# Gated mix of two state-space layers: work on GpSimd, VectorE and the DMA queues moved at three edges of the kernel

## The chip, the cores and the metric

The kernel runs on one core of a Trainium2 chip. TensorE multiplies matrices, VectorE and ScalarE work on tiles, GpSimd (POOL in the profile) works on tiles too and issues DMAs that add into their target, and SyncE (SP) issues the plain and the transposing DMAs. Each of them runs its own instructions in order. The metric is the device time of one execution in microseconds (us); lower is better. The kernel before took a median of 427.84 us over three runs (427.82 to 430.52).

## The reference

x is one sequence of 2048 rows and 1024 columns in bf16. The result is `g * a + (1 - g) * b`, where g is a gate per row, a is a linear recurrence over time with 1024 complex states, and b is a long convolution per column.

```python
g = sigmoid((x * gate_w).sum(-1, keepdims=True))

# a: the recurrence
dt = exp(log_dt); Lam = Lambda_re + 1j * Lambda_im
Lam_bar = exp(dt * Lam)
B_bar = ((Lam_bar - 1.0) / Lam)[:, None] * Bmat
Bu = einsum("bld,pd->blp", x, B_bar)
for t in range(L):
    h = Lam_bar * h + Bu[:, t, :]
a = 2.0 * einsum("blp,dp->bld", hseq, Cmat).real + x * Dskip

# b: the convolution (q is x here)
k_shift = sum over t of k_pad[:, t:t + S, :] * shift_k[:, ks - 1 - t]      # ks = 4
kv = k_shift * v
y = irfft(rfft(kv, 2 * S) * rfft(ssm_k, 2 * S))[:, :S, :] + kv * ssm_D
b = x * y

out = g * a + (1 - g) * b
```

## The kernel before, in words

**The convolution** is done for one block of 128 columns at a time, c from 0 to 7 (`NC` is 8), as matrix products with cosine and sine tables. For one c:

- `load` puts k (transposed, tile `kT`), the long filter (`kn`) and v into SBUF, by SyncE's queue.
- `taps` makes the four-tap sums on TensorE, and ScalarE copies them to `ks`. `times_v` multiplies by v on VectorE, mirrors the result on TensorE, copies the mirror to `lo` on ScalarE, makes the difference `ev` on VectorE and the sum by a DMA from GpSimd's queue that adds `lo` into `ks` (line 485). `first_times_v` does the same for c = 0 with VectorE alone. `fold_K` does it for the filter.
- `fwd_K` and `fwd_V` transform both, in two halves `hf`; ScalarE copies the results to `Kh` and `Vh`.
- `products` multiplies the two spectra on VectorE into the tile `G`. It is a generator that is advanced by hand: step 1 writes the first product into `G`; step 2 makes `n1` and adds it into `G` by a DMA from GpSimd's queue (line 544); step 3 makes `t2`; step 4 makes and adds the others; step 5 adds the last `n1` into `G`, and needs the DMA's result; the rest finishes `G`. p0 is half 0, p1 is half 1, whose last steps run in the next c.
- `inverse` multiplies `G` with the tables `CI` and `SI` on TensorE (`psz`); ScalarE copies the result to `cv`, and SyncE stores it to a scratch buffer in DRAM.

The tables `CI` and `SI` come from `inverse_angles` and `inverse_table`, in two halves; each half of the table is three large ScalarE instructions (Abs, Sin, Sin).

**The factors of the states.** `state_params` (lines 330 to 385) makes the decay, the angles, the sines and cosines and the complex factor `c2r`, `c2i` of each state, on tiles of 128x8. `turn_table` then makes one table of turns per block of 128 states, in steps: ScalarE scales a row of times by the angle (`hr`), VectorE reduces it in two operations, ScalarE takes sine and cosine (`TCS`), then scales them into `m` (one buffer, `m_pool`) and into `TCSi`, and a DMA of GpSimd's queue adds `m` to `TCSi`.

**The recurrence** runs on blocks of 512 times (tb from 0 to 3) and groups of 256 states (g from 0 to 3). `Bu` multiplies x (transposed, tiles `xT`, one for each tb) with `BT[g]` on TensorE. `scan` turns it with `TCSi` (`A`), runs the decay with VectorE's scan instruction (`W`), and turns back (`hb`). `Cy` multiplies `hb` with `CT` into a row block of 128 times (`psy`), and `scale_a` scales that by the gate on ScalarE. `loads` fetches the convolution's result (`pbb`) and x (`xr`) for a row block, `scale_b` scales `pbb` and makes `gd` from `drow` (Dskip on all partitions), which a DMA adds to `pbb`. `finish` multiplies the two on VectorE, adds the scaled `psy` and stores the rows. The last four row blocks have their sums of `Cy` over g interleaved, since all need the last scan.

**Order.** `put` chains every instruction behind the one that was put on the same engine before, so the order on each engine is the order of the Python text. PSUM holds four tiles of 128x1024, used in turn (`ps2`): TensorE can start a tile when the one four places before has been read. What the change touches is in three places: the loop over c for c = 0 (with the lines just ahead of it), the loop's last turn with the stage for c = 7 that follows, and the last four row blocks.

SyncE's queue, in order, around the second place: `xT` of block 1 (two transposes, line 813), `BT[2]` (two), the two stores of `cv`, `drow` (line 875), `BT[3]` (two), the stores of `inverse(6)`, of `inverse(7)`, `xT` of block 2, 16 transposes for `CT`, then the first `loads`.

Of the kernel before, what the change touches and what calls it, by code (L numbers as in the profile page):

```python
# [9 lines left out]
ALU = mybir.AluOpType  # L10
# [10 lines left out]
def kernel(  # L21
# [71 lines left out]
    def put(eng, f, *a, **kw):  # L93
        with tc.issue_after(prev[eng]) if eng in prev else nullcontext():
            i = f(*a, **kw)  # L95
        prev[eng] = getattr(i, "ins", i)
# [9 lines left out]
    def tt(o, a, b, op):  # L106
        put("dve", V.tensor_tensor, out=o, in0=a, in1=b, op=op)

    def ts(o, a, s1, s2, op0, op1=None):
        if op1 is None:  # L110
            put("dve", V.tensor_scalar, out=o, in0=a, scalar1=s1, scalar2=None, op0=op0)
        else:
            put("dve", V.tensor_scalar, out=o, in0=a, scalar1=s1, scalar2=s2, op0=op0, op1=op1)

    def copy(o, a):
        put("dve", V.tensor_copy, o, a)
# [213 lines left out]
    def state_params():  # L330

        dtv = small("dtv")
        act(dtv, logdt, func=ACT.Exp)
        av = small("av")
        tt(av, dtv, Lre, ALU.mult)
        bv = small("bv")
        tt(bv, dtv, Lim, ALU.mult)
        act(rv, av, func=ACT.Exp)
        ts(thn, bv, 1.0 / TWO_PI, None, ALU.mult)
        yield  # L340
        thU = small("thU")
        ts(thU, thn, float(TB), None, ALU.mult)
        frs = []
        for x, name in ((thn, "th"), (thU, "thU")):
            rq = small(name + "_rq")
            ts(rq, x, MAGIC, -MAGIC, ALU.add, ALU.add)
            fr = small(name + "_fr")
            tt(fr, x, rq, ALU.subtract)
            frs.append(fr)
        sc = []  # L350
        for fr, name in zip(frs, ("th", "thU")):
            fa = small(name + "_fa")
            act(fa, fr, func=ACT.Abs)
            s_ = small(name + "_sin")
            act(s_, fr, func=ACT.Sin, scale=TWO_PI)
            c_ = small(name + "_cos")
            act(c_, fa, func=ACT.Sin, bias=pih, scale=-TWO_PI)
            sc += [s_, c_]
        sth, cth, cs["sU"], cs["cU"] = sc
        yield  # L360
        rc = small("rc")
        tt(rc, rv, cth, ALU.mult)
        rs = small("rs")
        tt(rs, rv, sth, ALU.mult)
        nre = small("nre")
        ts(nre, rc, -1.0, None, ALU.add)
        den = small("den")
        tt(den, Lre, Lre, ALU.mult)
        den2 = small("den2")
        tt(den2, Lim, Lim, ALU.mult)  # L370
        tt(den, den, den2, ALU.add)
        invden = small("invden")
        put("dve", V.reciprocal, invden, den)
        ts(invden, invden, 2.0, None, ALU.mult)
        t_a = small("t_a")
        t_b = small("t_b")
        tt(t_a, nre, Lre, ALU.mult)
        tt(t_b, rs, Lim, ALU.mult)
        tt(t_a, t_a, t_b, ALU.add)
        tt(c2r, t_a, invden, ALU.mult)  # L380
        tt(t_a, rs, Lre, ALU.mult)
        tt(t_b, nre, Lim, ALU.mult)
        tt(t_a, t_a, t_b, ALU.subtract)
        tt(c2i, t_a, invden, ALU.mult)
        ts(mc2i, c2i, -1.0, None, ALU.mult)

    def turn_table(pi, home):

# [86 lines left out]
    def times_v(c):  # L475

        ks, v = kss[c], lds.pop(("v", c))
        tt(ks, ks, v.rearrange("p (b q) d -> p q b d", q=4), ALU.mult)
        yield
        lo = eo_pool.tile([128, 2, 4, 128], BF16, name="lo")  # L480
        act(lo, mirror(c), func=ACT.Copy)
        yield
        e = eo_pool.tile([128, 2, 4, 128], BF16, name="ev")
        tt(e, ks[:, 2:4], lo, ALU.subtract)
        gather(ks[:, 2:4], lo)
        eos["v", c] = e, ks[:, 2:4]

    def fwd_K(c, hf):
# [32 lines left out]
            act(Vp[:, :, :, f2], ps, func=ACT.Copy, scale=2.0 / 1024.0)  # L521
        VH[c, hf] = Vp

    def products(c, hf, home=u4):

        K, Vt = KH.pop((c, hf)), VH.pop((c, hf))
        G = g_pool.tile([128, 2, 4, 2, 128], BF16, name="G")

        def mult(a, k, home=w4, t=None):

            full = [128, 2, 4 - a, 256]
            if t is None:
                t = home(full, BF16, "t")
            Ka = K[:, k:k + 1, a:a + 1].rearrange("p c b f d -> p c b (f d)")
            tt(t, bc(Ka, full), Vt[:, :, 0:4 - a].rearrange("p c b f d -> p c b (f d)"), ALU.mult)
            return t

        def at(a):
            return G[:, :, a:4].rearrange("p c b f d -> p c b (f d)")

        mult(0, 0, t=at(0))
        yield
        n1 = mult(1, 0, home)
        gather(at(1), n1)
        yield
        t2 = mult(0, 1, home)
        yield
        n2 = mult(1, 1)
        n3 = mult(2, 1)
        tt(t2[:, :, 1:], t2[:, :, 1:], n2, ALU.add)  # L550
        n2 = mult(3, 1)
        tt(t2[:, :, 2:], t2[:, :, 2:], n3, ALU.add)
        n1 = mult(2, 0)
        n3 = mult(3, 0)
        tt(t2[:, :, 3:], t2[:, :, 3:], n2, ALU.add)
        tt(n1[:, :, 1:], n1[:, :, 1:], n3, ALU.add)
# [136 lines left out]
        act(gd, drow, func=ACT.Identity, scale=gcols[:, t_:t_ + 1])  # L693
        gather(pbb, gd)

    def Cy_g(tb, tl, ps, g, last, js=range(2)):
        tsl = slice(tl * 128, (tl + 1) * 128)
        for j in js:
            for c in range(2):
                for dh in range(2):  # L700
                    mm(ps[dh], hbs[tb, g][:, c, j, tsl], CT[2 * g + j][:, c, dh * 512:(dh + 1) * 512],
                       g == 0 and j == 0 and c == 0, last and j == 1 and c == 1)
# [18 lines left out]
    def finish(t_, ps=None):  # L721

        rows = slice(t_ * 128, (t_ + 1) * 128)
        pbb, xr = ios.pop(t_)
        tt(xr, xr, pbb, ALU.mult)
        if t_ < NT - 4:
            ga = gas.pop(t_)
            gather(ga, xr)
            yield
        elif ps is None:  # L730
            yield
            ga = gas.pop(t_)
            tt(ga, ga, xr, ALU.add)
        else:
            yield
            ga = a_room(t_)
            for o, i in ps:
                put("dve", V.scalar_tensor_tensor, out=ga[:, o], in0=i, scalar=gcols[:, t_:t_ + 1], in1=xr[:, o],
                    op0=ALU.mult, op1=ALU.add)
        move(of[rows, :], ga)  # L740


    def step(gen):
        next(gen, None)
# [43 lines left out]
    run(turns)  # L788
    run(inverse_angles(1))
    turns = inverse_table(1)  # L790
    p0 = products(0, 0)
    steps(p0, 3)
    tv = times_v(1)
# [8 lines left out]
    for c in range(NC - 1):  # L802
# [5 lines left out]
        if c < 4:  # L808
            load_BT(c // 2, c % 2)
        elif c < 6:  # L810
            load_xT(0, halves=(c - 4,))
        else:
            load_xT(1)
            load_BT(2, 0)
            load_BT(2, 1)
        tabs = turn_table(c - 1, u4) if c else none
        back = inverse(c - 1) if c else none
        if c:
# [5 lines left out]
            run(p1)  # L824
            steps(p0, 2)
            run(tv)
        p1 = products(c, 1)

        fwd_K(n, 0)
        step(p0)  # L830
        if c == 0:
            run(tv)
        if nn < NC:
# [11 lines left out]
        run(p0)  # L845
        if nn < NC:
            taps(nn, dg)
        if c == 0:
            step(sp)
        step(tabs)  # L850
        fwd_K(n, 1)
        step(p1)
        if c == 0:
            run(sp)
        fwd_V(n, 0)
        if nn < NC:
            run(fold_K(nn))
            tv = times_v(nn)
            step(tv)
        if c == 0:  # L860
            run(turns)
        fwd_V(n, 1)
        old = tabs

# [2 lines left out]
    with tc.tile_pool(name="fin", bufs=1, side="right") as fin:  # L867
# [4 lines left out]
            return fin.tile(shape, dt, name=name, tag=f"fin{next(count)}")  # L872

        p0, back = products(c, 0, room), inverse(c - 1)
        move(drow, bc(A_Dskip.rearrange("(o d) -> o d", o=1), [128, D]))
        load_BT(3, 0)
        load_BT(3, 1)
        ta, tb_ = turn_table(NP - 2, room), turn_table(NP - 1, room)
# [17 lines left out]
        step(tb_)  # L896
        run(tb_)
        step(p0)
        p1 = products(c, 1, room)
        steps(p1, 2)  # L900
        step(p0)
        step(p1)
        run(p0)
        Bu(0, 1)
        run(p1)
        Bu(0, 2)
# [13 lines left out]
    load_xT(2, xt2_pool)  # L920
    for pi in range(NP):
        load_CT(pi)
    loads(0)
    Bu(0, 3)
    Bu(1, 0)
# [39 lines left out]
    pss = []  # L965
    for tl in range(4):
        ps = ps2([128, 2, 512], "psy")
        pss.append(([ps[:, 0], ps[:, 1]], [(slice(0, D), flat(ps))]))
    for g in range(NG - 1):
        for tl in range(4):  # L970
            Cy_g(tb, tl, pss[tl][0], g, False)
    run(finish(t0 - 1))
    fins = []
    for tl in range(4):
        fins.append(finish(t0 + tl, pss[tl][1] if tl % 2 else None))
        step(fins[tl])
    for tl in range(4):
        Cy_g(tb, tl, pss[tl][0], NG - 1, False, [0])
    for tl in range(4):
        Cy_g(tb, tl, pss[tl][0], NG - 1, True, [1])  # L980
        if tl % 2 == 0:
            scale_a(t0 + tl, pss[tl][1])
    for tl in (1, 0, 3, 2):
        run(fins[tl])
# [1 line left out]
_INS = ['A_x', 'A_Lambda_re', 'A_Lambda_im', 'A_B_re', 'A_B_im', 'A_C_re', 'A_C_im', 'A_log_dt', 'A_Dskip', 'B_q', 'B_k', 'B_v', 'B_shift_k', 'B_ssm_k', 'B_ssm_D', 'gate_w']  # L986
# [26 lines left out]
```

## Time and profile before

The profiled execution took 431.18 us, with a span of 429.4 us from the first to the last instruction; the granted clock was 1.00.

| | busy us | share of the span | instructions |
|---|---|---|---|
| TensorE matmul (PE) | 411.8 | 96% | 2375 |
| VectorE (DVE) | 403.3 | 94% | 577 |
| ScalarE (ACT) | 249.1 | 58% | 303 |
| GpSimd (POOL) | 61.5 | 14% | 80 |

| stage, us from the start | what runs |
|---|---|
| 0 to 50 | tables, first column block, factors of the states |
| 50 to 184 | the loop over column blocks |
| 184 to 214 | last column block, last tables, first `Bu` |
| 214 to 416 | scans on VectorE, `Bu` and `Cy` on TensorE |
| 416 to 429 | last row blocks |

How to read the views: a line of the timeline has start, length, engine, source line, operation, what it writes and reads, and in brackets the idle time of its engine before it and what ended it. Nearly all instructions carry line 95, that of `put`, so they are told apart by their tiles. A line of the waits has who waited for whom, total us, times and the longest. Matmuls are issued every 0.21 us while each lasts 0.38, so TensorE at 9.95 of 10 us is full. POOL's DMA lines show the making of the DMA, not the transfer; a DMA's landing is read from its semaphore.

### The profile page before, as it was taken

Reading aid. Unit: us, or ns where it says so; the run is one execution under the profiler, and the core shown is the slowest. Engines: PE = TensorE matmul, PEld = TensorE weight load, DVE = VectorE, ACT = ScalarE, POOL = GpSimd, SP = SyncE. Lnnn points to the kernel's source line nnn. Section 1 sums busy time; section 2 is a strip of 40 time slices with the busy share of each in tenths; the row PEclk is TensorE's granted clock in tenths of the full one; section 3 lists DMA queues with packets and bytes.
Section 4 is the critical chain, followed back from the end, with each engine's and each line's share of the span. In section 5 each row is a group of like instructions: output and inputs, shape, how many; then the busy total and the mean of one; then the engine's idle time right before and its main releaser. Section 6 shows DMA issues by size and latency. Waiting matters only on the chain.

```text
span 429.4 us, 6238 instructions
## 1 busy us (share of the span) xinstructions
PE 411.8 (96%) x2375; PEld 205.0 (48%) x2413; DVE 403.3 (94%) x577; ACT 249.1 (58%) x303; POOL 61.5 (14%) x80
## 2 busy tenths in 40 slices
PE   8898899999999998899999999999999999999995
PEld 5455364645446463344445444444444444444442
DVE  8899899979999996979999999999999999999973
ACT  5696969797979886687523335234332433477002
POOL 3011120211212110301100001010101110223100
PEclk9999999999999999999999999999999999999999
DMA  7779978899698899895339991245674656388413
GB/s 148 148 151 140 165 159 150 182 154 196 128 196 172 157 220 141 145 170 115 61 102 189 180 216 26 44 105 123 139 180 86 135 140 154 56 202 170 112 26 123
DMA packets 134353, 60.20 MB, mean 140 GB/s; under 512 B 118442, under 2 KB 122546, under 8 KB 134323
## 3 DMA queue, kind: packets, MB, share of 16 engines
q1 hardware_dynamic: 123696, 42.22, 48.5%
q0 software_dynamic: 10544, 17.57, 25.6%
q8 instruction: 19, 0.31, 0.3%
q14 instruction: 12, 0.09, 0.1%
q10 hardware_dynamic: 82, 0.02, 0.0%
HBM read 12.86 MB, written 8.39 MB: 49 GB/s over the span
## 4 chain that ended last, share of the span: by engine, by line
DVE 30%; PE 24%; DMA 5%; issue 4%; ACT 1%; DVEq 0%; ACTq 0%
PE psy L95 17%; DVE W L95 9%; PE bu L95 6%; DVE t L95 5%; DVE trn L95 4%; DVE A L95 4%; DVE hb L95 4%; DMA G<-t 3%; DVE G L95 2%; DMA TCSi<-m 2%; DVE hr L95 1%; DVE BT L95 0%; DVE xr L95 0%; PE p L95 0%; ACT TCSi L95 0%
## 5 line engine op out<-in xcount | busy, mean ns | idle before, releaser
L95 PE MATMUL psy<-CT,hb 128*128 128x512 bf16 x502 | 111.8, 379 | 0.9 <-DVE hb L95 0.3
L95 PE MATMUL bu<-xT,BT 128*128 128x512 bf16 x499 | 111.6, 379 | 0.6
L95 DVE TENSOR_TENSOR t<-Kh,Vh 128x1536 bf16<-128x1536 bf16 (+3 forms) x112 | 81.6, 758 | 0.0
L95 PEld LDWEIGHTS <-hb 128*128 128x128 bf16 x512 | 49.7, 98 | 60.8 <-DVE hb L95 1.3
L95 PEld LDWEIGHTS <-BT 128*128 128x128 bf16 x512 | 50.0, 98 | 60.3 <-issue 0.2
L95 ACT ACTIVATE U<-bu 128x1024 bf16<-128x1024 f32 x32 | 32.5, 1020 | 49.5 <-PE bu L95 44.7
L95 DVE TENSOR_TENSOR_SCAN W<-rv,init,A 128x512 bf16<-128x512 f32 x48 | 57.7, 1262 | 0.0
L95 PE MATMUL psz<-G,CI 128*128 128x512 bf16 x128 | 48.5, 379 | 1.7 <-DVE G L95 1.6
L95 PE MATMUL psz<-G,SI 128*128 128x512 bf16 x128 | 48.5, 379 | 0.7 <-DVE G L95 0.7
L95 DVE TENSOR_TENSOR G<-G,t 128x1024 bf16<-128x1024 bf16 x48 | 31.5, 682 | 8.9 <-DMA G<-t 8.8
L95 DVE TENSOR_TENSOR t<-t 128x1536 bf16<-128x1536 bf16 (+1 forms) x64 | 38.1, 615 | 0.0
L95 ACT ACTIVATE ga<-psy,gcols 128x1024 bf16<-128x1024 f32 x8 | 8.9, 1113 | 47.0 <-PE psy L95 47.0
L95 POOL DMA_DIRECT2D G<-t x16 | 20.5, 1284 | 103.7 <-DVE t L95 79.6
L95 ACT ACTIVATE Kh<-psk 128x1024 bf16<-128x1024 f32 x32 | 31.7, 1040 | 1.7 <-PE psk L95 1.5
L95 ACT ACTIVATE Vh<-psv 128x1024 bf16<-128x1024 f32 x32 | 31.2, 1047 | 1.5 <-PE psv L95 1.5
L95 PE MATMUL taps<-dg,kT 128*128 128x128 bf16 x512 | 31.8, 225 | 0.0
L95 PEld LDWEIGHTS <-kT 128*128 128x128 bf16 x512 | 30.9, 101 | 1.6
L95 ACT ACTIVATE cv<-psz 128x1024 bf16<-128x1024 f32 x16 | 16.4, 1023 | 23.1 <-PE psz L95 23.0
L95 POOL DMA_DIRECT2D pbb<-gd x12 | 10.3, 860 | 125.9 <-ACT gd L95 114.0
L95 ACT ACTIVATE BT<-psy,gcols 128x1024 bf16<-128x1024 f32 x6 | 6.7, 1109 | 30.9 <-PE psy L95 30.9
L95 PE MATMUL psk<-eok,SF 128*128 128x512 bf16 (+1 forms) x95 | 24.0, 361 | 0.4
L95 PEld LDWEIGHTS <-SF 128*128 128x128 bf16 x160 | 15.6, 98 | 17.2 <-issue 2.0
(137 smaller groups left out, 575.7 us busy)
## 6 DMA issues: line engine op xcount, KB each, us to landing
G<-t POOLq DMA_DIRECT2D x16, 384.0 KB, 6.3
v<-in_B_v_dram SPq DMA_DIRECT2D x8, 512.0 KB, 5.3
cv_scr<-cv SPq DMA_DIRECT2D x16, 256.0 KB, 3.5
pbb<-cv_scr SPq DMA_DIRECT2D x12, 256.0 KB, 3.6
xr<-in_A_x_dram SPq DMA_DIRECT2D x12, 256.0 KB, 3.5
pbb<-gd POOLq DMA_DIRECT2D x12, 256.0 KB, 3.4
TCSi<-m POOLq DMA_DIRECT2D x8, 256.0 KB, 4.4
ga<-xr POOLq DMA_DIRECT2D x8, 256.0 KB, 3.6
```

The lines of the kernel that those rows point to most:

```text
L95: i = f(*a, **kw)
```

## The change

At the start (c = 0): sixteen of the seventeen last operations of `state_params` go from VectorE to GpSimd (`ptt`, `pts`); the reciprocal stays. Its second step, which makes the reduced angles on VectorE, is now ahead of products(0,0), and the sines and cosines are a step of their own. The three ScalarE instructions of the inverse table's second half run at three places of the turn instead of one after another behind `fold_K`. For c = 1 the sum of `ks` and `lo` is done by VectorE.

At the end of the convolution: the transposes for `xT` of block 1 are issued behind the stores of `inverse(6)`, `drow` behind the transposes for `CT`. The addition of `n1` in products(6,1) and products(7,1) is done by VectorE, in step 4.

At the end: the last group's products of a row block are done at one go. Of the last four row blocks the second is scaled by ScalarE, the others by VectorE as they are added; the last one is added and stored in two halves of 512 columns.

```diff
+    def ptt(o, a, b, op):
+        put("pool", nc.gpsimd.tensor_tensor, out=o, in0=a, in1=b, op=op)
+
+    def pts(o, a, s1, op):
+        put("pool", nc.gpsimd.tensor_scalar, out=o, in0=a, scalar1=s1, scalar2=None, op0=op)
...
             frs.append(fr)
+        yield
         sc = []
...
-        tt(rc, rv, cth, ALU.mult)
+        ptt(rc, rv, cth, ALU.mult)
         rs = small("rs")
-        tt(rs, rv, sth, ALU.mult)
+        ptt(rs, rv, sth, ALU.mult)
...
         put("dve", V.reciprocal, invden, den)
-        ts(invden, invden, 2.0, None, ALU.mult)
+        pts(invden, invden, 2.0, ALU.mult)
...
-        gather(ks[:, 2:4], lo)
+        if c == 1:
+            tt(ks[:, 2:4], ks[:, 2:4], lo, ALU.add)
+        else:
+            gather(ks[:, 2:4], lo)
...
-    def products(c, hf, home=u4):
+    def products(c, hf, home=u4, by_dma=True):
...
-        gather(at(1), n1)
+        if by_dma:
+            gather(at(1), n1)
         yield
         t2 = mult(0, 1, home)
         yield
         n2 = mult(1, 1)
+        if not by_dma:
+            tt(at(1), at(1), n1, ALU.add)
...
             for o, i in ps:
                 put("dve", V.scalar_tensor_tensor, out=ga[:, o], in0=i, scalar=gcols[:, t_:t_ + 1], in1=xr[:, o],
                     op0=ALU.mult, op1=ALU.add)
+                if len(ps) > 1:
+                    move(of[rows, o], ga[:, o])
+            if len(ps) > 1:
+                return
...
     turns = inverse_table(1)
+    step(sp)
     p0 = products(0, 0)
...
         else:
-            load_xT(1)
             load_BT(2, 0)
...
-        p1 = products(c, 1)
+        p1 = products(c, 1, by_dma=c < NC - 2)
         fwd_K(n, 0)
         step(p0)
+        step(turns)
...
             taps(nn, dg)
+        step(turns)
         if c == 0:
             step(sp)
...
         step(p1)
+        run(turns)
         if c == 0:
             run(sp)
...
-        if c == 0:
-            run(turns)
         fwd_V(n, 1)
...
-        move(drow, bc(A_Dskip.rearrange("(o d) -> o d", o=1), [128, D]))
         load_BT(3, 0)
...
-        p1 = products(c, 1, room)
+        p1 = products(c, 1, room, False)
         steps(p1, 2)
         step(p0)
         step(p1)
         run(p0)
+        load_xT(1)
         Bu(0, 1)
...
         load_CT(pi)
+    move(drow, bc(A_Dskip.rearrange("(o d) -> o d", o=1), [128, D]))
     loads(0)
...
+        halves = [(slice(h * 512, h * 512 + 512), ps[:, h]) for h in range(2)]
+        pss.append(([ps[:, 0], ps[:, 1]], halves if tl == 3 else [(slice(0, D), flat(ps))]))
...
-        fins.append(finish(t0 + tl, pss[tl][1] if tl % 2 else None))
+        fins.append(finish(t0 + tl, None if tl == 1 else pss[tl][1]))
         step(fins[tl])
     for tl in range(4):
-        Cy_g(tb, tl, pss[tl][0], NG - 1, False, [0])
-    for tl in range(4):
-        Cy_g(tb, tl, pss[tl][0], NG - 1, True, [1])
-        if tl % 2 == 0:
+        Cy_g(tb, tl, pss[tl][0], NG - 1, True)
+        if tl == 1:
             scale_a(t0 + tl, pss[tl][1])
-    for tl in (1, 0, 3, 2):
         run(fins[tl])
```

More of the change, by code (lines that the diff above doesn't have):

```diff
@@ L361, in state_params @@
         rc = small("rc")
-        tt(rc, rv, cth, ALU.mult)
+        ptt(rc, rv, cth, ALU.mult)
         rs = small("rs")
-        tt(rs, rv, sth, ALU.mult)
+        ptt(rs, rv, sth, ALU.mult)
         nre = small("nre")
-        ts(nre, rc, -1.0, None, ALU.add)
+        pts(nre, rc, -1.0, ALU.add)
         den = small("den")
-        tt(den, Lre, Lre, ALU.mult)
+        ptt(den, Lre, Lre, ALU.mult)
         den2 = small("den2")
-        tt(den2, Lim, Lim, ALU.mult)
-        tt(den, den, den2, ALU.add)
+        ptt(den2, Lim, Lim, ALU.mult)
+        ptt(den, den, den2, ALU.add)
         invden = small("invden")
         put("dve", V.reciprocal, invden, den)
-        ts(invden, invden, 2.0, None, ALU.mult)
+        pts(invden, invden, 2.0, ALU.mult)
         t_a = small("t_a")
         t_b = small("t_b")
[L377 to L385, printed above, removed]
+        ptt(t_a, nre, Lre, ALU.mult)
+        ptt(t_b, rs, Lim, ALU.mult)
+        ptt(t_a, t_a, t_b, ALU.add)
+        ptt(c2r, t_a, invden, ALU.mult)
+        ptt(t_a, rs, Lre, ALU.mult)
+        ptt(t_b, nre, Lim, ALU.mult)
+        ptt(t_a, t_a, t_b, ALU.subtract)
+        ptt(c2i, t_a, invden, ALU.mult)
+        pts(mc2i, c2i, -1.0, ALU.mult)
     def turn_table(pi, home):
@@ L694, in scale_b, with Cy_g @@
         gather(pbb, gd)
-    def Cy_g(tb, tl, ps, g, last, js=range(2)):
+    def Cy_g(tb, tl, ps, g, last):
         tsl = slice(tl * 128, (tl + 1) * 128)
-        for j in js:
+        for j in range(2):
             for c in range(2):
@@ L967 @@
         ps = ps2([128, 2, 512], "psy")
-        pss.append(([ps[:, 0], ps[:, 1]], [(slice(0, D), flat(ps))]))
+        halves = [(slice(h * 512, h * 512 + 512), ps[:, h]) for h in range(2)]
+        pss.append(([ps[:, 0], ps[:, 1]], halves if tl == 3 else [(slice(0, D), flat(ps))]))
     for g in range(NG - 1):
```

## The prediction

> **What bounds the kernel now.** I read the page's slices and its chain of waits first. TensorE (PE) is 96% busy and VectorE (DVE) 94%, so neither share names the bound. The chain in order of time does; its columns are start, length (us) and what ran:
>
> ```profile
> 154.23 12.50 DMA G<-t
> ...
> 178.28 9.58 DMA TCSi<-m
> ...
> 309.69 1.13 DVE A L95
> 310.82 1.22 DVE hb L95 x2
> 312.04 7.05 PE psy L95 x32
> ...
> 407.72 8.22 PE psy L95 x38
> ```
>
> Two accumulating DMAs, then VectorE up to 312.0, then TensorE without a break to its last matmul at 424.29. From about 191 to 416 VectorE has no idle stretch over 0.12, so whatever VectorE saves before 213 (its first scan, of A, starts at 214.0) reaches 312 whole. TensorE passes it on to the end, since after 312 it waits for nobody and the change leaves its matmuls the same. TensorE must keep up before 312, and there I look at who waits (total us, times, longest):
>
> ```profile
> DVE G L95 <- DMA G<-t: 8.8, 3, 4.1
> DVE ev L95 <- ACT lo L95: 1.6, 1, 1.6
> PE psz L95 <- DVE G L95: 2.3, 5, 1.4
> PE psv L95 <- ACT Kh L95: 1.6, 1, 1.6
> PE psv L95 <- DMA ks<-lo: 1.5, 1, 1.5
> PE psk L95 <- ACT Vh L95: 1.2, 1, 1.2
> ```
>
> These lie in two places, 41 to 53 us and 162 to 193 us. The timelines of the engines there show why:
>
> ```profile
> 31.84 0.90 POOL L95 DMA_DIRECT2D ks<-lo  x1 [6.72 <-DVE dg L95]
> 42.76 0.59 PE L95 MATMUL psv<-ks,SF 128*128 128x512 bf16 x2 [1.54 <-DMA ks<-lo]
> 51.31 0.38 PE L95 MATMUL psk<-eok,CF 128*128 128x512 bf16 x1 [1.17 <-ACT Vh L95]
> 152.74 7.03 SPq L95 DMA_TRANSPOSE xT<-in_A_x_dram  x2
> 159.81 6.78 SPq L95 DMA_TRANSPOSE BT<-in_A_B_re_dram  x1
> 166.82 0.69 DVE L95 TENSOR_TENSOR G<-G,t 128x1024 bf16<-128x1024 bf16 x1 [4.13 <-DMA G<-t]
> 179.51 0.63 ACT L95 ACTIVATE hr<-hr 128x512 f32<-128x512 f32 x1 [1.52 <-DVE hr L95]
> 187.95 0.72 ACT L95 ACTIVATE m<-TCS,c2i 128x512 bf16<-128x512 bf16 x1 [1.20 <-DMA TCSi<-m]
> 190.15 0.69 DVE L95 TENSOR_TENSOR G<-G,t 128x1024 bf16<-128x1024 bf16 x1 [2.04 <-DMA G<-t]
> ```
>
> The gather-add of n1 into G took 12.50 beside three transposes, against a median of 6.3; VectorE stood 4.13, and TensorE, ScalarE and TensorE again paid behind it.
>
> **Part 1, 20 to 53 us.** *The sum of ks and lo for c = 1 by VectorE.* One more 128x1024 bf16 add, 0.68 by the row of ev, 0.60 from start to start; TensorE's 1.54 for the DMA (landed 10.9 after issue) goes. *The five thU and frs operations* go ahead of products(0,0), where VectorE idles 0.54 for Kh, and cost 0.72 - 0.54 = 0.2, which its 0.35 wait for ks at 24.5 covers; if that cover were gone, 0.2. *Inverse table.* Its three ACT instructions (1.05, 1.05, 1.14), now in a block at 47.3, are spread. The first fills ACT's 0.76 wait for taps at 35.2; the second stands before the six small ones and Kh(1,1); the third before Vh(1,0). Adding up ACT from the end of ks at 38.82: 1.05 + 0.9 + 2 x 1.0 (Kh) + 1.14 + 1.94 (Vh) + 2.0 (eok) + 1.95 (Vh) = 49.8, against 52.2 now: what it saves is its 1.54 wait at 43.39 and the 0.76. TensorE, whose PSUM tiles come free in that order, then waits about 0.3, 0.15 and 0.6 and starts psz at 50.8 instead of 52.83: 2.03 earlier. lo ends at 50.8 rather than 53.1.
>
> *The factors.* Sixteen of 17 small VectorE operations (42.90 to 45.39, 2.49 in all) go to GpSimd; the reciprocal stays and now waits for six GpSimd operations, which wait for ACT's th_cos (about 40.4 in the new order). VectorE comes to it at 42.6. Behind it in VectorE's queue stand ks times v, the sums of G(0,1) and the first products of c = 1; TensorE's mirror and psz wait for those. VectorE would reach ev at 48.9 and wait for lo until 50.8, so 1.9 of delay at the reciprocal is free: it costs from six operations of (44.5 - 40.4) / 6 = 0.68 each. Behind the other ten stand kT's memset (needed by taps near 58) and the gather of G(1,0). What GpSimd takes for such an operation no row shows. Nearest rows:
>
> ```profile
> L209 POOL IOTA colf_i<- 128x4 int32 x1 | 0.1, 133 | 0.0
> L209 POOL IOTA row_i<- 128x512 int32 x1 | 1.1, 1080 | 0.0
> L209 POOL IOTA fr__i<- 128x512 int32 x1 | 0.6, 558 | 0.0
> L256 POOL TENSOR_SCALAR_AFFINE_SELECT refl<-refl 128x128 bf16<-128x128 bf16 x2 | 1.0, 520 | 0.0
> ```
>
> For 128x8 I take 0.25, between the 0.13 of a tiny iota and the 0.52 of a 128x128 operation that also reads, nearer the tiny one in size; ends 0.13 and 1.5. The upper end comes from the two 512-element iotas: 1.08 while VectorE ran full f32 work (a two-input one in part) and 0.56 while it hardly worked, so an operation may also have to sit out a VectorE one (longest 1.22). At 0.25 den is ready at 41.9 and the whole chain costs nothing.
>
> Part 1: TensorE 2.03, VectorE 2.3; I count 2.05 (ends 0 and 2.3; a loss is the first rival). From 53 to 160 TensorE shows one wait, 0.5 at 117.5, so the schedule shifts as it stands.
>
> **Part 2, 150 to 213 us.** *xT1 later.* Its two 512 KB transposes leave SP's queue ahead of BT2's two and go behind the cv stores of inverse(6), near 200. So BT2's move up from 159.8 to 152.7 and have flowed, as xT1's did, before G's transfer gets going: TCSi's gather ahead of it landed at 160.04. G then runs alone: 384 KB, median 6.3, best 4.4; 160.0 plus half of that gives 162.5, when VectorE arrives (162.69). I take a remaining wait of 0.1 (ends 0 and 4.13): VectorE 4.0 earlier, TensorE 1.9 (its psz waits of 1.39 and 0.22, and pipeline), ACT's 1.52 for hr goes, and with it most of TensorE's 1.59 for Kh: TensorE 3.0.
>
> *drow later* (behind CT; needed by scale_b near 258, landing near 253): TCSi's gather at 178.28 took 9.58 behind cv, drow and BT3. Without drow the queue looks as at 153.68 (cv, two transposes), where it took 6.36. ACT's m then waits for nothing: its Vh end 3.0 earlier, m starts 4.15 earlier (1.2 + 3.0), and with it hr, which VectorE's next step needs. VectorE itself, without the 2.04 wait, would be there at 185.6; so hr, at 186.8 instead of 190.97, ends last: 4.15. If TCSi's gather stays at 9.58, 2.0.
>
> *Sums by VectorE in products(6,1) and (7,1).* Each adds a 128x1536 bf16 add, 0.95 (0.87 start to start). The first lies in the 1.2 that VectorE still waits for hr; cover gone, 0.87 more. The second lies bare ahead of the scans: 0.87.
>
> *xT1 near 200* meets the gather of TCSi(6) (landed 203.50, ACT waited 2.17) and delays ACT by up to about 3; the U copies behind it are due before inverse(7) at 212, so nothing. Bu(1,0) reads xT1 at 227; issued at 200 and with xT's longest landing, 10.4, twice over it would still be there by 221.
>
> Part 2: 4.15 - 0.87 = 3.3 (ends 0.3 and 3.6).
>
> **Part 3, the last rows.** Matmuls are the same, whole tiles one after another; they need the last hb at 412.9, TensorE comes at 417.4. Tiles 0 to 2 now finish beside TensorE. Behind the last matmul lay 1.28 + 0.60 of VectorE and a 256 KB store issued at 426.37; now two halves of about 0.75 (1.28 less 512 elements) and the last store of 128 KB at 425.9. I take 0.5 (ends 0.3 and 0.8).
>
> **Sum.** 2.05 + 3.3 + 0.5 = 5.85. The profiled execution took 431.18 around a span of 429.4, so I expect 423.6 of span and 425.3 there; against the median of 427.84, **422.0**. A difference under 1% (4.28) is what I count as no change.
>
> **The rivals.**
> 1. *GpSimd starves beside VectorE, and the kernel is slower.* At x us per operation the reciprocal is 6x - 4.05 late, and the gather of G(1,0), behind all sixteen, lands at 47.2 + 16x while VectorE wants it at 59.3: together 16x - 12.1, of which VectorE's 2.6 wait at 93 takes up 2.65. It eats the 5.85 from x = (12.1 + 2.65 + 5.85) / 16 = 1.29. With 1.22 for a VectorE operation sat out and 0.25 of its own, x = 1.47: 11.4 - 2.65 - 5.85 = 2.9 slower, 430.7. For it: VectorE is full of two-input operations there. Against: kT's memset took 0.10 at 37.9 beside them.
> The Trainium skill (GPSIMD Engine Reference, Key points) says that GpSimd "Shares its SBUF interfaces with VectorE" with contention when a VectorE instruction has two SBUF inputs. By that rule it is this rival; the two iotas fit, the memset, which reads nothing, can't tell.
> 2. *BT2's transposes hold the gather as xT1's did.* VectorE gains nothing at 162, only TCSi's earlier landing (1.2) less 0.87: 2.05 + 0.3 + 0.5 = 2.85, 425.0. For it: G's transfer was slow beside BT2 in particular, from 160 on. Against: BT2 starts 7 earlier.
> 3. *ACT's pieces only move the wait:* Kh(1,1) comes 1.2 later and TensorE waits there what it waited before. Part 1 is 0: 424.0.
>
> **How the numbers follow.** Forecast 0.57, own range 420.5 to 423.5; rival 1 0.12; rival 2 0.18; rival 3 0.13. The lowest, with all upper ends, is 427.84 - 2.3 - 3.6 - 0.8 = 421.1, less 0.6 for the spread of a run: 420.5. Upward 2 and 3 together give 427.0; I stop at 426.0, which leaves out rival 1 and part of that. Faster by over 1% (below 423.56): 0.58, the forecast and a little of rival 3. Slower: 0.11. Within: 0.31.
>
> **What would show it.** Right: no TensorE wait near 42 and 51; reciprocal within 1 of the VectorE operation before it; G's gather of c = 5 under 9 to land, VectorE's wait there under 1; the TCSi gather that is now issued at 178 near 6.4; VectorE's first scan step 5 earlier, at 209; 1.6 from last matmul to last store instead of 2.1. Wrong: sixteen GpSimd spans of over 0.7; a gather of 12 again; TensorE's psk or psv waiting over 1 between 38 and 50.

## The result, and the profile after

The changed kernel took 424.88 us (median of 22 runs, 423.27 to 430.88) against 428.37 for the kernel before in the same job (22 runs): a ratio of 0.993, 95% interval 0.9902 to 0.9959, that is 1.8 to 4.2 us faster where 5.85 was forecast. (Medians here are of all runs; the ratios leave out, on both sides, runs over 1.5% above the fastest of their kernel.) Its profiled execution took 424.63 us around a span of 422.9.

What VectorE and TensorE wait for in it (lists of waits of the changed kernel; total us, times, longest):

```profile
DVE G L95 <- DMA G<-t: 2.8, 1, 2.8
...
DVE invden L95 <- POOL den L95: 1.1, 1, 1.1
```
```profile
PE psz L95 <- DVE G L95: 0.6, 2, 0.4
...
PE psk L95 <- ACT eok L95: 0.3, 1, 0.3
```

VectorE's 8.8 us of waiting for the gather-adds have become 2.8, one wait near 93 that was there before (2.65 at 95). TensorE's waits for Kh, Vh and the DMA of ks are gone. New is the reciprocal's wait for GpSimd. The timeline of GpSimd in the changed kernel (start us, us, operation) shows why:

```profile
40.77 2.51 POOL L95 TENSOR_TENSOR rc<-rv,th_cos 128x8 f32<-128x8 f32 x1 [3.85 <-ACT thU_fa L95]
43.25 0.19 POOL L95 TENSOR_TENSOR rs<-rv,th_sin 128x8 f32<-128x8 f32 x1
43.43 0.24 POOL L95 TENSOR_SCALAR nre<-rc 128x8 f32<-128x8 f32 x1
43.65 0.34 POOL L95 TENSOR_TENSOR den<-pcol 128x8 f32<-128x8 f32 x2
44.07 0.20 POOL L95 TENSOR_TENSOR den<-den,den 128x8 f32<-128x8 f32 x1
44.60 1.11 POOL L95 TENSOR_SCALAR invden<-invden 128x8 f32<-128x8 f32 x1 [0.33 <-DVE invden L95]
45.67 0.60 POOL L95 TENSOR_TENSOR t_a<-nre,pcol 128x8 f32<-128x8 f32 x1
46.23 1.18 POOL L95 TENSOR_TENSOR t_b<-rs,pcol 128x8 f32<-128x8 f32 x1
```

and beside it VectorE's (the same kernel and view):

```profile
42.46 0.76 DVE L95 TENSOR_TENSOR t<-t 128x512 bf16<-128x512 bf16 x2
44.30 0.20 DVE L95 RECIPROCAL invden<-den 128x8 f32<-128x8 f32 x1 [1.08 <-POOL den L95]
44.42 1.19 DVE L95 TENSOR_TENSOR ks<-ks,v 128x2048 bf16<-128x2048 bf16 x1
45.52 0.68 DVE L95 TENSOR_TENSOR G<-G,t 128x1024 bf16<-128x1024 bf16 x1
46.12 1.23 DVE L95 TENSOR_TENSOR G<-Kh,Vh 128x2048 bf16<-128x2048 bf16 x1
```

A 128x8 operation takes 0.19 to 0.24 while VectorE stands at the reciprocal, and 0.53 to 1.18 (the ten later ones, not all shown) beside its two-input operations; the first took 2.51 and ended (43.28) just after VectorE fell idle (43.22). Each of these eleven slow ones ends 0.06 to 0.10 after an instruction of VectorE ends, as 46.27 after 46.20 and 47.41 after 47.35. Why the first was kept out over five such ends is not shown. The Trainium skill (GPSIMD Engine Reference, Key points) has GpSimd share its SBUF interfaces with VectorE, in contention, among other cases, when a VectorE instruction has two SBUF inputs; the trace agrees in these rows.

In the stretch of 150 to 195 us the chain that ended last, which went through two late gathers before, now has none (the chain of waits of the changed kernel: start, length, what ran):

```profile
164.75 6.92 PE psz L95 x32
171.66 0.02 issue
171.69 1.03 ACT cv L95
...
183.13 0.62 ACT hr L95
183.75 0.02 issue
183.77 0.47 DVE hr L95
184.24 1.20 DVE G L95 x2
```

Both marks moved: TensorE's first psz from 52.83 to 50.70, VectorE's first scan from 214.03 to 207.67, the last matmul from 424.29 to 417.94. From the first scan to the last matmul it is 210.25 to 210.27 us in every profiled execution of this study, whatever the kernel. So 6.4 us came out ahead of the scans, in these two executions; the medians differ by 3.5. That gap is the question.

### The profile page after: what moved, and what is told of

Its sections match the earlier page's. It is cut to its first block, busy times and chain, and to the rows that moved or that the text cites. A ratio compares the mean times of both kernels' runs of the same rounds, so it can differ in the third digit from the quotient of the medians.

```text
span 422.9 us, 6276 instructions
## 1 busy us (share of the span) xinstructions
PE 413.3 (98%) x2413; PEld 205.5 (49%) x2413; DVE 404.4 (96%) x565; ACT 247.7 (59%) x302; POOL 69.2 (16%) x93
## 4 chain that ended last, share of the span: by engine, by line
PE 68%; DVE 22%; DMA 4%; ACT 3%; issue 1%; DVEq 0%; ACTq 0%; SPq 0%
PE psy L95 25%; PE bu L95 13%; PE psz L95 8%; PE psk L95 8%; DVE t L95 6%; PE taps L95 6%; DVE W L95 4%; PE psv L95 3%; DVE G L95 3%; DVE A L95 3%; PE foldk L95 3%; DMA G<-t 2%; DVE trn L95 2%; DMA BT<-in_A_B_re_dram 1%; DVE hb L95 1%
## 5 line engine op out<-in xcount | busy, mean ns | idle before, releaser
L95 DVE TENSOR_TENSOR t<-Kh,Vh 128x1536 bf16<-128x1536 bf16 (+3 forms) x112 | 83.2, 776 | 0.0
L95 ACT ACTIVATE U<-bu 128x1024 bf16<-128x1024 f32 x32 | 32.6, 1023 | 50.3 <-PE bu L95 47.8
L95 PE MATMUL psz<-G,CI 128*128 128x512 bf16 x128 | 48.5, 379 | 0.4 <-DVE G L95 0.4
L95 PE MATMUL psz<-G,SI 128*128 128x512 bf16 x128 | 48.5, 379 | 0.2 <-DVE G L95 0.2
L95 DVE TENSOR_TENSOR t<-t 128x1536 bf16<-128x1536 bf16 (+1 forms) x64 | 39.0, 635 | 0.0
L95 DVE TENSOR_TENSOR G<-G,t 128x1024 bf16<-128x1024 bf16 (+1 forms) x50 | 34.0, 710 | 3.0 <-DMA G<-t 2.8
L95 POOL DMA_DIRECT2D G<-t x14 | 17.9, 1276 | 89.7 <-DVE t L95 78.4
L95 PE MATMUL psk<-eok,CF 128*128 128x512 bf16 (+1 forms) x96 | 25.5, 361 | 0.3 <-ACT eok L95 0.3
```

## The experiments

Theory 1: the parts do what the prediction says, but the DMA waits between 53 and 214 us differ by several us from one execution to the next; the one profiled execution of before had large ones, and a sum of them can't be taken off the median. Theory 2, its rival: those waits belong to the kernel before in every execution, and the changed kernel gives about 3 us back somewhere in its usual executions, which its profile did not catch. The third batch adds theory A (transposes on SyncE's queue slow the gather-adds on GpSimd's; the change only put others beside them), B (the gather of TCSi ahead on the same queue does) and C (another late DMA always takes the place of the one removed).

All runs in one table. "psz" is the start of TensorE's first psz; "work" and "waits" are what VectorE does and waits (stretches over 0.13) from its first ev after 49 us to its first scan; "G(5,1)" is the time from issue to landing of the gather-add of n1 into G for c = 5, second half. The last four columns are from one profiled execution each; the ratio is to the kernel before in the same job. The experiments ran in three jobs: before_again to end_only, after_again to sums_dma, and the last four. The kernel before had medians of 426.97, 427.69 and 428.42 in them.

| run | median us | ratio, 95% interval | psz | work | waits | G(5,1) |
|---|---|---|---|---|---|---|
| before | 428.37 | 1 | 52.83 | 152.1 | 8.8 | 12.5 |
| the change | 424.88 | 0.993 [0.9902, 0.9959] | 50.70 | 153.8 | 3.4 | 8.0 |
| before_again | 427.50 | 1.0016 [0.9988, 1.0043] | 55.02 | 151.9 | 5.6 | 10.2 |
| start_only | 425.26 | 0.9959 [0.9935, 0.9984] | 50.44 | 152.0 | 6.1 | 11.0 |
| mid_only | 428.47 | 1.0032 [0.9998, 1.0066] | 52.52 | 153.7 | 5.1 | 10.0 |
| end_only | 427.79 | 1.0029 [1.0006, 1.0052] | 51.69 | 152.1 | 6.2 | 7.2 |
| after_again | 424.94 | 0.9942 [0.992, 0.9964] | 50.03 | 153.6 | 4.7 | 6.5 |
| sum21_dve | 424.43 | 0.9921 [0.9887, 0.9955] | 50.40 | 154.6 | 2.1 | 7.8 |
| factors_dve | 424.91 | 0.9931 [0.9898, 0.9964] | 49.66 | 153.7 | 6.7 | 13.8 |
| sums_dma | 424.24 | 0.9929 [0.9893, 0.9966] | 50.35 | 152.1 | 5.4 | 10.4 |
| bt2_later | 424.11 | 0.9934 [0.9892, 0.9976] | 49.81 | 153.6 | 3.5 | 5.1 |
| best_bt2 | 423.46 | 0.9887 [0.9854, 0.992] | 50.12 | 153.7 | 2.7 | 5.1 |
| best_sums | 423.33 | 0.99 [0.9865, 0.9934] | 50.46 | 153.6 | 3.0 | none |
| before_third | 430.04 | 1.0036 [0.9996, 1.0077] | 52.69 | 152.1 | 8.1 | 7.6 |

**before_again**: the kernel before, unchanged.

> The kernel before, unchanged, profiled a second time. Theory 1 (the profiled execution of before, 431.18 us against a median of 428.37, had longer DMA waits than a usual one, and the forecast subtracted them from the median): with a time near 428 here, VectorE's wait for the gather-add of G(5,1) near 160 us is about 1 to 2 us instead of 4.13, that for G(6,1) near 188 is 2 or less, and the first scan starts near 211 to 212 instead of 214.0. Theory 2 (the waits of before are always there, and the changed kernel gives back about 3 us in most executions, its own profile being a good one): the wait near 160 is 4 us again, the first scan at 214, whatever the time. Ratio to before 1.000, within 0.003.

Its waits were 2.42, 1.78 and 1.25 for G instead of 2.65, 4.13 and 2.04. The code is the same, and so is VectorE's work, to 0.2 us. That fits theory 1, which missed two things: the execution took 430.04, not near 428, and the first scan came at 212.87, not by 212, because psz started 2.2 later. The reason is one more late DMA, the one that adds `lo` into `ks` for c = 1. TensorE stood 2.48 us for it where the first profile has 1.54, and then ran at half the clock for a while, as a line of its timeline and two of the table by stretches show (stretch, sum, PE, PEld, DVE, ACT, POOL busy, clock, DMA share, GB/s):

```profile
43.46 1.01 PE L95 MATMUL psv<-ks,SF 128*128 128x512 bf16 x2 [2.48 <-DMA ks<-lo]
```
```profile
44.00:46.00 2.00, 2.00 (x7) 0.64 (x5) 1.83 (x8) 1.02 (x1) 0.00 (x0) 0.50 1.28 146
47.00:50.00 3.00, 3.00 (x15) 1.09 (x13) 2.73 (x4) 2.68 (x4) 0.00 (x0) 1.00 0.05 12
```

The granted clock was 0.50 for 3.41 us, two matmuls took 1.01 instead of 0.59, and by 48.5 TensorE was 2.2 behind the first profile. In the fourteen traces there is one other such place ahead of the last matmul, in factors_dve: 0.50 for 3.41 us again, behind a stand of 2.72. TensorE's other stands are all of 1.9 us or less, with the clock at 1.00 behind them.

**start_only**: only the part from 20 to 53 us.

```diff
-        tt(rc, rv, cth, ALU.mult)
+        ptt(rc, rv, cth, ALU.mult)
...
+        if c == 1:
+            tt(ks[:, 2:4], ks[:, 2:4], lo, ALU.add)
+        else:
+            gather(ks[:, 2:4], lo)
...
+        step(turns)
```

> Only the edits at the start: factors on GpSimd, inverse table in pieces, second step of the factors earlier, sum of ks and lo for c = 1 by VectorE. Both theories: first psz at 50.9 instead of 52.8, TensorE's waits near 42 and 51 gone. Theory 1: this shift reaches the end whole, 2.0 us, ratio 0.995. Theory 2: part of what is lost is lost here (GpSimd's operations take 0.5 to 1.2 us beside VectorE): ratio 0.997 to 1.000.

The ratio 0.9959 is 0.7 to 2.8 us of 427; the interval holds theory 1's 0.995 and the lower end of theory 2's range. psz starts at 50.44, near the changed kernel's 50.70.

**mid_only**: only the moves of xT1 and drow and the two sums by VectorE.

```diff
-            load_xT(1)
             load_BT(2, 0)
...
-        p1 = products(c, 1)
+        p1 = products(c, 1, by_dma=c < NC - 2)
...
-        move(drow, bc(A_Dskip.rearrange("(o d) -> o d", o=1), [128, D]))
```

> Only the edits near the end of the convolution: transposes of xT block 1 and drow later, sums of n1 by VectorE for (6,1) and (7,1). Theory 1: in a usual execution there is little to remove; the first scan starts near 210.5 in this one and the time falls 0.5 to 1.5 us, ratio 0.997 to 0.999. Forecast as it was made: 3.3 us, ratio 0.992. Theory 2: first scan near 210 in the profile, yet ratio 0.997 to 1.000.

No gain: 1.0032, above all three forecasts, and even the lower end of the interval leaves only 0.1 us; the first scan came at 211.58. In its profile VectorE has 1.65 more of work and 1.9 less of waits than the five executions with the middle of before have on average (152.05 and 6.95; before, before_again, before_third, start_only, end_only). Its gather of G(5,1), now beside BT2's transposes, took 10.0.

**end_only**: only the last rows.

```diff
-        Cy_g(tb, tl, pss[tl][0], NG - 1, False, [0])
-    for tl in range(4):
-        Cy_g(tb, tl, pss[tl][0], NG - 1, True, [1])
-        if tl % 2 == 0:
+        Cy_g(tb, tl, pss[tl][0], NG - 1, True)
+        if tl == 1:
             scale_a(t0 + tl, pss[tl][1])
```

> Only the edits of the last four row blocks. Both theories: from the last matmul to the last store's issue 1.6 us instead of 2.1; 0.5 us less, ratio 0.999. If the halves or the order cost something, ratio above 1.000.

A miss: no gain shows, and the ratio even reads slower. In the profile the time from the last matmul to the end of the span is 4.88 us, against 5.10 to 5.12 in the executions with the old end. The three partial kernels shared one job, in which before read 426.97 and its twin before_again 427.50; the product of their ratios, 1.002, does not give the whole's 0.993, and against the twin it is 0.997. From medians, the sum of the parts is therefore known only to some 2 us; what each part does is read from the profiles.

**after_again**: the changed kernel, unchanged.

> The changed kernel, unchanged, profiled a second time. Theory 1 (what varies from execution to execution is VectorE's waits for gather-adds between 50 and 210 us; the rest of the kernel is the same each time): from the first scan to the last matmul 210.27 us again, VectorE's own work from ev of c = 2 to the first scan 153.8 us, and all difference in time is the sum of its waits for G; first psz at 50.7 within 0.2. Theory 2 (the changed kernel loses about 3 us elsewhere in a usual execution): another stretch than these waits is longer. Ratio to before 0.993 within 0.003.

424.94 against 424.88, and both profiled executions (424.63 and 425.10) lie at these medians; so theory 2's usual execution, which gives 3 us back, is not seen. One wait for G fell on the same gather as in the first execution (2.35 near 92, there 2.79), the other (2.37 at 139) on one for which nobody had waited. Theory 1 missed here too: psz came at 50.03, not at 50.7, and G's waits, 1.9 us more in sum, made the execution only 0.5 longer, since the earlier psz, no wait for hr and 0.2 less of work took the rest.

**sum21_dve**: the change, and one more sum by VectorE.

```diff
-        p1 = products(c, 1, by_dma=c < NC - 2)
+        p1 = products(c, 1, by_dma=c < NC - 2 and c != 2)
```

> The changed kernel with n1 of products(2,1) added by VectorE too. Theory 1: VectorE's wait near 90 us (1.1 to 3.4 in six executions) goes for 0.87 of work, so the first scan comes 0.3 to 2.5 earlier than in the changed kernel and the time falls about 1.5 us: ratio 0.989 to 0.991. If TensorE bounded that stretch, the wait would be idle time that costs nothing, and the kernel would be 0.9 slower or the same: 0.993 to 0.995.

The wait near 92 is gone, 0.65 came at 114, 0.34 at 159 and 1.09 for hr at 183; work rose by the 0.87. The median is 0.5 lower than after_again's in the same job, with intervals that overlap, and the ratio, 0.9921, lies between the two forecasts: not told apart.

**factors_dve**: the change, with the sixteen small operations on VectorE again.

```diff
-        put("pool", nc.gpsimd.tensor_tensor, out=o, in0=a, in1=b, op=op)
+        put("dve", V.tensor_tensor, out=o, in0=a, in1=b, op=op)
```

> The changed kernel with the sixteen small operations back on VectorE, all else as changed. Theory 1: VectorE has 2.25 us more work and no 1.08 wait at the reciprocal; ev of c = 2 starts 1.2 later (51.7 instead of 50.5), TensorE's first psz stays near 50.7, and the kernel is 1.2 us slower than the changed one: ratio 0.996. Rival (GpSimd's slow operations and VectorE's wait for them give back what they save, since lo from ScalarE comes no earlier than 50.4): ev within 0.3 of 50.5, ratio 0.993.

424.91, beside after_again's 424.94 in the same job: no gain from moving them to GpSimd shows, though the interval would still hold theory 1's 0.996. The profile is nearer to the rival. VectorE's ev comes at 50.67, within the 0.3 that the rival allowed, though after those of all kernels with the operations on GpSimd (49.61 to 50.50, on average 50.1); TensorE's psz comes at 49.66, before all of those (49.81 to 50.70), for a reason that is not shown. This execution also holds the worst gather of all. Its chain of waits and the table by stretches (stretch, sum, PE, PEld, DVE, ACT, POOL busy, clock, DMA share, GB/s):

```profile
150.35 13.83 DMA G<-t
164.18 0.03 issue
```
```profile
152.00:154.00 2.00, 2.00 (x12) 1.08 (x11) 2.00 (x4) 2.00 (x5) 0.00 (x0) 1.00 1.25 225
154.00:156.00 2.00, 2.00 (x11) 0.88 (x9) 2.00 (x5) 2.00 (x3) 0.00 (x0) 1.00 1.29 226
156.00:158.00 2.00, 2.00 (x10) 0.70 (x9) 2.00 (x6) 2.00 (x3) 0.00 (x0) 1.00 1.29 60
158.00:160.00 2.00, 2.00 (x11) 0.89 (x10) 0.78 (x1) 2.00 (x4) 0.00 (x0) 1.00 1.74 93
160.00:162.00 2.00, 2.00 (x12) 1.03 (x11) 0.00 (x0) 2.00 (x4) 0.00 (x0) 1.00 1.09 44
162.00:164.00 2.00, 2.00 (x11) 0.81 (x9) 0.00 (x0) 2.00 (x3) 0.00 (x0) 1.00 0.60 95
```

From 156 to 162 the DMA engines are as busy as before (share over 1) and move less than a third of what they did: 44 to 93 GB/s. VectorE stands from 158.8 on. From 156 on BT2's two transposes are the only other large transfer in flight, the ones that the prediction took to have flowed before G's transfer gets going.

**sums_dma**: the change, with the sums in products(6,1) and (7,1) by the DMA as before; xT1 and drow stay later.

```diff
-        p1 = products(c, 1, by_dma=c < NC - 2)
+        p1 = products(c, 1)
...
-        p1 = products(c, 1, room, False)
+        p1 = products(c, 1, room)
```

> The changed kernel with n1 of products(6,1) and (7,1) added by DMA again, transposes of xT block 1 and drow still later. Theory 1: VectorE's work from ev to the first scan falls from 153.8 to 152.0; a wait of 0.5 to 2 for G(6,1) beside BT's transposes comes back, and one of 0 to 2 for G(7,1) beside xT's; ratio 0.991 to 0.994, no clear difference to the changed kernel. As forecast (the waits worth 2.04 and more): slower than the changed kernel by over 1 us, ratio 0.996 or more.

Work is 152.1 again; the wait that comes back is 0.3 at 206 and none at (6,1), whose gather took 6.8 us instead of 8.1 to 11.2 in the kernels with drow beside it. So in this kernel that wait is gone without the adds, most likely by the later drow, and the two adds of 0.87 are mostly paid for nothing. The median is 0.7 under after_again's, intervals overlapping.

**bt2_later**: BT2's loads out of the way of the gather.

```diff
-        else:
-            load_BT(2, 0)
-            load_BT(2, 1)
...
+        load_BT(2, 0)
+        load_BT(2, 1)
         load_BT(3, 0)
```

> The changed kernel with one more move: the two loads of BT2 leave the place near 150 us (where the gather-add of n1 into G for c = 5 is in flight) and go just ahead of those of BT3, near 173. Theory A (the gather is slow because transposes share its queues' engines; the change only put BT2's transposes where xT1's had been, so its slowness stayed): without any transpose beside it the gather lands in 4.4 to 6.0 us, as the gather of c = 6 did that ran alone (4.4), VectorE has no wait for it near 162, and the median is 1 to 2 us under the changed kernel's, 423 to 424. Theory B (it is slow for what runs ahead of it on its own queue, the gather of TCSi): it still takes 7 or more, and the median stays at 424.9. In both the TCSi gather near 174 keeps a pair of transposes beside it and stays near 5; VectorE's own work from its first ev to its first scan stays 153.7 us plus waits, and from the first scan to the last matmul 210.27.

The timeline of SyncE's queue in the changed kernel, then in bt2_later (its line of 22.99 puts three stores together, issued at 149.1, 168.3 and 171.8):

```profile
150.43 1.79 SPq L95 DMA_TRANSPOSE BT<-in_A_B_re_dram  x1
152.28 6.98 SPq L95 DMA_TRANSPOSE BT<-in_A_B_im_dram  x1
```
```profile
149.09 22.99 SPq L95 DMA_DIRECT2D cv_scr<-cv  x3
172.12 1.96 SPq L95 DMA_TRANSPOSE BT<-in_A_B_re_dram  x1
174.12 3.78 SPq L95 DMA_TRANSPOSE BT<-in_A_B_im_dram  x1
```

With no transpose beside it the gather landed in 5.06 us, and in 5.06 again in best_bt2 (by tile G, 150 to 156 us, the changed kernel and then bt2_later):

```profile
DMA to landing us min/median/max: 8.0/8.0/8.0
```
```profile
DMA to landing us min/median/max: 5.1/5.1/5.1
```

Beside xT1's, and in most of these executions BT2's too, it took 12.5, 10.2, 11.0, 7.2 and 7.6 (mean 9.7), beside BT2's alone 8.0, 10.0, 6.5, 7.8, 13.8 and 10.4 (mean 9.4). The gather of TCSi stands ahead of it on GpSimd's queue in all thirteen, so theory B falls.

The packets in the traces show two parts of the delay. In ten of the eleven executions with transposes (in the eleventh another gather is still in flight) the first packet of the two gathers comes 3.1 to 4.4 us after the issue of TCSi's, while SyncE's queue moves 0.6 to 0.8 MB; in the two without them it comes after 1.4. From there to the landing of G, both gathers (640 KB) take 4.2 us without transposes, 4.2 in the changed kernel and 10.9 in factors_dve. The Trainium skill (DMA: Bandwidth & Descriptors, Queues, rings and completion order) has each DMA engine take packets from its queues in turn; the second part, with packets of both queues in the same microseconds, agrees with that, the first does not show it, and sharing alone would not cut the sum of both to 44 GB/s. What causes either is open. The median, 424.11, is 0.8 under the change's in another job; by it the expected 1 to 2 can't be confirmed.

**best_sums** and **best_bt2**: VectorE adds only where gathers are late.

```diff
-        p1 = products(c, 1, by_dma=c < NC - 2)
+        p1 = products(c, 1, by_dma=c not in (2, 5))
...
-        p1 = products(c, 1, room, False)
+        p1 = products(c, 1, room)
```

That is best_sums; best_bt2 is bt2_later with `c < NC - 2 and c != 2` in the first line and the same second edit.

> The changed kernel with other sums of n1 by VectorE: those of products(2,1) and (5,1), whose gathers are the late ones, in place of those of (6,1) and (7,1). VectorE's own work stays 153.7 us. Waits: none near 92 and none near 162 (in the five executions of kernels with BT2 in that place they were 0.0 to 5.5 at 162, mean 2.1, and 1.2 to 3.4 at 92), up to 1 each near 188 and 206. Theory A and B alike: 422 to 423.5. Theory C (another late DMA takes their place): 424.5 to 425.

> bt2_later, with the sum of n1 in products(2,1) made by VectorE (one more add of 0.87 us, for a wait of 1.2 to 2.8 near 92) and that in products(7,1) given back to the DMA (0.87 less, for a wait of 0.0 to 0.3). Theory A: about 0.9 from the first and 0.6 to 0.9 from the second, on top of bt2_later: 421.5 to 422.5, and the span of the profiled execution near 420. Theory B: only these two, 423.0 to 423.5. If the waits only move on to the next gather (as theory C has it, by which the schedule always finds another late DMA), 424 to 425.

423.33 and 423.46: both lie about 1.5 under the changed kernel's medians, which are from other jobs, and the first meets its 422 to 423.5. best_bt2 misses its 421.5 to 422.5, with a span of 421.5 instead of 420: the waits did partly move, as theory C has it, in best_sums too (0.72 at 114, 1.43 for hr at 183, 0.81 at 205). VectorE's list of waits in best_bt2:

```profile
DVE G L95 <- DMA G<-t: 1.5, 2, 0.9
...
DVE hr L95 <- ACT hr L95: 1.1, 1, 1.1
```

More telling than the medians is the spread: all 11 runs of best_bt2 lie in 423.14 to 424.99 and all 8 of best_sums in 422.81 to 424.58, while even the quicker half of the 30 runs of before in that job spreads from 425.7 to 428.4. bt2_later, in the same job, has nine runs up to 424.8 and three above 427. That fits theory 1: with the late gathers taken away, little is left that varies. It is not proof, since what the runs without a profile waited for is not known.

**before_third**: the kernel before, a third profile.

> The kernel of before unchanged, a third profiled execution: VectorE's waits for G's gathers near 95, 166 and 190. If the waits of 2.65, 4.13 and 2.04 that the prediction subtracted were one draw of a wide spread, it shows others, with 158 to 160 us from TensorE's first psz to VectorE's first scan (the five executions of kernels with the middle of before had 161.2, 157.9, 158.5 and 157.9); if they belong to the kernel, near 161. The median is that of before, 427 to 428.5, either way.

Its waits are 2.45, 1.79 and 3.81, the second at a place (142) where no other execution of before waits, none at 166. Its chain of waits:

```profile
164.16 3.03 DVE G L95 x4
...
177.24 9.74 DMA TCSi<-m
186.98 0.02 issue
```

Same code, other waits: theory 1. Its median, 430.04, is above the 427 to 428.5 expected, with 12 runs from 425.96 to 437.82; so far do medians of the same code differ. And from psz to the first scan it took 160.5, near the 161.2 that it was to show if the waits were fixed; the spread, 157.9 to 161.2, has both ends in executions of before.

## Why the prediction was wrong

**The step that failed is the last of the sum**: "so I expect 423.6 of span and 425.3 there; against the median of 427.84, 422.0". For the execution that it was worked out on, the sum held: 425.3 forecast, 424.63 and 425.10 in the two profiles of the changed kernel. But that execution, at 431.18, stood 3.3 over the median, and it had waits of 8.8 us in the stretch of Part 2, the most of the five executions with the middle of before (8.8, 8.1, 6.2, 6.1, 5.6; mean 6.95). So 1.9 of the 3.3 are waits that a usual execution has not and that can't be saved in it; where the rest of the 3.3 lies is not shown. The term of the sum that this makes too large is Part 2.

**Part 2, 3.3 forecast.** About 0.3 on average: VectorE's waits went from 6.95 (those five) to 4.97 (mid_only, the change, after_again, factors_dve: 5.1, 3.4, 4.7, 6.7), its work from 152.0 to 153.7. That is the lower of the ends given. With so few executions the 0.3 is known to about 1 us, but 3.3 is excluded by mid_only, too. By place, 2.4 fewer are waited near 188 and 0.1 near 162, 0.5 more ahead of 155, and 1.65 go into the adds. By its own steps:
- "G then runs alone", a remaining wait of 0.1: false. The second rival had it right: BT2's transposes hold the gather as xT1's did, 9.4 against 9.7 us, and VectorE waits 1.74 there on average (0, 1.64, 0, 0.34, 5.5, 2.93) instead of 1.85 (4.13, 1.78, 0, 3.32, 0). Its 425.0 is where the time came out, by luck in the sizes: it had 1.2 - 0.87 where the executions have the four terms above. bt2_later shows the mechanism, 5.06 without transposes. Luck also made the sign named for being right appear, a gather under 9 with a wait under 1: in the changed kernel's profile it took 8.0 beside BT2's and nobody waited, in mid_only 10.0, in factors_dve 13.8.
- drow later: right. The gather of TCSi near 175 took 5.0 to 5.4 instead of 8.4 to 9.7, and the wait behind it (2.04, 1.25, 3.81, 0.89, 4.40 in the five) is gone; hr is the next bound, as the prediction had it: 0.58 to 1.43 in the six executions with the later drow in which VectorE waits for it.
- Sums by VectorE: the price of the two adds was right (1.65 measured, twice 0.87 forecast), the return small, as sums_dma shows.

**Part 1, 2.05 forecast.** psz comes at 50.3 on average over the eight executions with the new start (factors_dve apart), 52.95 over the five with the old (before, its two copies, mid_only, end_only): 2.65 earlier, a little over the upper end, or 2.1 without the 55.02 of before_again with its half clock; start_only's ratio, 0.7 to 2.8 us, agrees. Here too a DMA that varies was taken off: TensorE's wait for ks, 1.54 in the first profile, was 2.48, 1.76 and 0.98 in three other executions with the old start and under 0.2 in end_only. In the changed kernel's profile Kh, Vh and ks cost TensorE nothing any more and lo ends at 50.37, so the third rival falls. The first rival's mechanism was the right one and its price too high: beside VectorE the ten later operations took 0.78 on average, not 0.25 as I took nor the 1.29 from which it decides; the first six took 3.5 us together, 0.58 each against the 0.68 that was free. The gather of G(1,0) went out at 52.76 rather than 50.72 and nobody waited. The cover held; with the 0.25 I had it right for the wrong reason.

**Part 3, 0.5 forecast.** From last matmul to last store issue it went from 2.08 to 1.47, as forecast. From last matmul to the end of the span only from 5.12 to 4.92; over all, the old end has 5.10 to 5.12, the new 4.86 to 4.92: 0.2. The lines of the tail, from VectorE's timeline in the changed kernel:

```profile
416.28 1.28 DVE L95 SCALAR_TENSOR_TENSOR BT<-psy,gcols,BT 128x1024 bf16<-128x1024 f32 x1
417.98 1.41 DVE L95 SCALAR_TENSOR_TENSOR BT<-psy,gcols,BT 128x512 bf16<-128x512 f32 x2 [0.42 <-PE psy L95]
```

SyncE saw the last store landed at 421.12, 1.7 before the end of the span; before, at 428.48, 0.9 before the end. By the trace, SyncE then has seven more checks of semaphores to pass one after another, and before it had all others behind it by the last landing. That the saving went there is read from the two traces, not tried.

On these averages the three parts come to 2.65 + 0.3 + 0.2 = 3.15, against 3.5 between the medians.

## What to carry to other kernels

Before a wait is taken off a median, ask how far the profiled execution stands from that median, and profile the same kernel two or three times: here VectorE's work was the same in each to 0.2 us, and its waits for DMAs were not. The transfer that was slow beside another was cured by an empty queue beside it, not by a swap of its neighbour; and an add on the bounding engine is only worth its price where the DMA that it replaces is late in most executions.

## What the hardware showed

- A gather-add of 384 KB on GpSimd's queue, behind one of 256 KB, took 5.06 us without transposes on SyncE's, twice, and 6.5 to 13.8 beside two to four of them, in eleven executions; in the worst, both queues together moved 44 to 93 GB/s for 6 us where 225 went through just before.
- A 128x8 operation on GpSimd takes 0.19 to 0.24 us with VectorE idle, 0.53 to 1.18 beside VectorE's two-input bf16 operations, ending 0.06 to 0.10 after one of them ends, and one took 2.51.
- Three executions of one kernel differ in VectorE's DMA waits between two marks by 3 us (5.6 to 8.8) while its work there repeats to 0.2.
- Behind stands of TensorE of 2.48 and 2.72 us the granted clock was 0.50 for 3.41 us; behind stands of up to 1.9 it stayed at 1.00.
